# The transfers that place the transposed blocks of the probabilities: begun by GpSimd instead of SyncE

## The chip, the core and the metric

The kernel runs on one core of one Trainium2 chip. The metric is device time in microseconds from one launch. The core has TensorE (PE in the profile), VectorE (DVE), ScalarE (ACT), GpSimd (POOL) and SyncE (SP). Each of them works through its own list of instructions in order and waits on semaphores for what the others produce. Transfers (DMAs) are begun by one of these engines and are carried out by sixteen DMA engines.

## The reference

An attention over chunks of 64 positions is followed by two feed-forward blocks. All in float32.

```python
# q, k, v: (8 batches, 8 heads, 576 positions, 64); nine chunks of 64 positions each
scores = q_c @ k_c^T / sqrt(64)           # 64 x 64 for each chunk and head
attn = exp(scores - max) / (sum + 1e-9)
x = attn @ v_c                            # -> (4608 tokens, 512)
x = ((x @ w1) * (x @ w2)) @ w3 @ w_out    # d_ff 1024
h = x @ w_in                              # d_ff 2048
out = (max(h, 0) + alpha * min(h, 0)) @ w_out2
```

## The kernel before

The 4608 tokens are cut into nine blocks of 512 (`TB`). Attention is done in 18 units of 256 tokens (`u`, two for a block, each unit with 16 pairs of a head pair and a chunk). A matrix product is made of three passes over high and low halves of the operands (`mm3`), so that TensorE does three 128x128 by 512 matmuls for each tile. `proj1` makes the two products with w1 and w2 (into the PSUM banks `a` and `b`), `product` multiplies them, `proj_wc` multiplies by w3 and w_out, folded into one matrix, and sums in `acc`. The last stage (`proj2`, `proj_out`) is the second block.

Attention of the first six units stands in a start phase with an order written out by hand. From unit 6 on (`BLOCKS_FROM`) the units are placed between the projections, two units for each of six blocks of tokens, and each unit has four steps (`unit_steps`):

- `first`: 64 small matmuls for the scores (tile `sc`), their maximum on VectorE, the exponentials on ScalarE (tile `e`).
- `second`: sums, reciprocal and the scaling of `e` on VectorE.
- `third`: `attn_turn(u)`, then the loads of the next unit (`load_unit`, lines 243 and 253).
- `fourth`: 64 small matmuls with the values (`attn_values_by_chunk`, tile `xo`, out of `pt` and `v`), and copies of the result.

`attn_turn` transposes `e` on VectorE, which turns each 32x32 block in place (STREAM_TRANSPOSE, one instruction for the unit). The blocks then stand on the wrong partitions. Eight transfers from SBUF to SBUF, each 32 partitions by 512 float32 (64 KB), carry them to the tile `pt`, of which there is one buffer. For unit u the order on TensorE between the turn and `xo` is the three groups of twelve matmuls (`acc`, `a`, `b`) of the projections around it: for blocks 3 to 7, `third` is placed ahead of the projections of f = 1 or 5, `fourth` behind `proj1` of f = 2 or 6.

TensorE keeps its program order throughout. Before the change all of the kernel's transfers are begun by SyncE, in one list; a scheduler that works with its own estimates of time sets the order on that list. Besides the eight of the turn there are in the same stretch the loads of `qk` and `v` of the next unit, the raw weights of the second block (`raw<-in_w2nd`, line 153, 512 KB each), their converted halves written to memory (`w_dram<-wm`, line 193) and the sums of a block (`y_dram<-y`, line 423). In the lists of instructions a transfer begun by SyncE waits on, and counts up, one of eight semaphores DMAHW0 to DMAHW7 in turn.

Of the kernel before, what the change touches and what calls it, by code (L numbers as in the profile page):

```python
# [60 lines left out]
def tile_attention_moe_moe(ctx: ExitStack, tc: tile.TileContext, qkv: bass.AP, w12: bass.AP,  # L61
# [8 lines left out]
    nc = tc.nc  # L70
# [5 lines left out]
    D = 64  # L76
# [220 lines left out]
    def e_blocks(u):  # L297

        return un[u]["e"].rearrange("p j a h k -> p j (a h k)").rearrange("p k (n x) -> p k n x", n=16)
# [25 lines left out]
    def attn_turn(u):  # L325


        e = e_blocks(u).rearrange("p k n x -> p k (n x)")
        flat = e.rearrange("p k c -> p (k c)")
        dve.transpose(out=flat, in_=flat)  # L330
        pt = un[u]["pt"] = work.tile([P, 2, 4 * 2 * 2, D // 2], F32, tag="pt", name="pt", bufs=1)
        for c in range(2):
            for i in range(2):
                for k in range(2):
                    r, to = D * c + D // 2 * i, D * c + D // 2 * k
                    nc.sync.dma_start(out=pt[to:to + D // 2, i].rearrange("p n x -> p (n x)"), in_=e[r:r + D // 2, k])  # L336

    def attn_values_by_chunk(u):
        v, pt = un[u]["v"].rearrange("p j a (h d) -> p j a h d", h=2), un[u]["pt"]
# [149 lines left out]
    for step in STARTUP.split():  # L489
        kind, rest = step[0], [int(n) for n in step[1:].split(".")]  # L490
        n = rest[0]
# [34 lines left out]
    def unit_steps(u, cut):  # L526


        def first():
            attn_scores(u)  # L530
            attn_max(u)
            attn_exp(u, range(1 if cut else 2))

        def second():
            if cut:
                attn_exp(u, range(1, 2))
            attn_softmax(u)

        def third():
            attn_turn(u)  # L540
            if u + 1 < NU:
                load_unit(u + 1)

        def fourth():
            attn_values_by_chunk(u)
            attn_out(u, False)
            attn_out(u, True)
        return [first, second, third, fourth]
# [110 lines left out]
```

## Time and profile before

| | |
|---|---|
| median of three runs | 1506.35 us (1504.86 to 1507.29) |
| time of the profiled execution | 1505.47 us |
| its span, first to last instruction | 1503.7 us |
| TensorE busy | 1478.7 us, 98% of the span |
| VectorE, ScalarE busy | 805.8 us (54%), 409.2 us (27%) |
| GpSimd busy | 0.7 us, 6 instructions |
| transfers of the turn (`pt<-e`) | 96 of 64 KB, 12 units by 8 |
| stretch in which they lie | 241.6 to 631.2 us of the span |

The span is what the profile sees; the 1.8 us between it and the execution's time lie around it. Busy time of TensorE is modelled for pipelined matmuls, so what matters is where TensorE sat idle and what ended the idle time. In the views a start is in us from the start of the span, and a value in square brackets is the time that the engine was idle before the row, with what ended it. SPq is SyncE's list of transfers; the length of its rows is the time to begin them, not to move the data. Line 105 is a helper through which most compute instructions are recorded, so tiles are told apart by name.

### The profile page before, as it was taken

The page shows a single profiled execution, that of the slowest core. Times are in us where ns is not written, and L with a number is a line of the kernel's source. Part 1 is how long each engine was busy: PE and PEld are TensorE (multiplying, and loading weights), DVE is VectorE, ACT ScalarE, POOL GpSimd, SP SyncE. Part 2 cuts the span into 40 slices and gives each one's busy share as a digit, 9 for nine tenths or more (in the row PEclk, how much of TensorE's full clock was granted, in tenths as well). Part 3 has the DMA queues.
Part 4 walks back from the last instruction along what each step waited for, and adds up shares of the span by engine and source line. Part 5 has one row for each costly group of instructions (what it writes and reads, how often), then busy time and mean ns, then how long its engine had stood idle before and what let it go on. Part 6 is the DMA issues. An engine that isn't in the chain of part 4 may idle for free.

```text
span 1503.7 us, 21181 instructions
## 1 busy us (share of the span) xinstructions
PE 1478.7 (98%) x8592; PEld 1218.1 (81%) x8592; DVE 805.8 (54%) x1274; ACT 409.2 (27%) x1108; POOL 0.7 (0%) x6
## 2 busy tenths in 40 slices
PE   5999999999999999999999999999999999999998
PEld 4788887788888888888888888888888888888887
DVE  7999984376666666622434343443434344343433
ACT  6554334344443444321111111111111111111111
POOL 0000000000000000000000000000000000000000
PEclk9999999999999999999999999999999999999999
DMA  8544447465555555565201010000101000000000
GB/s 296 175 141 153 150 153 230 136 210 169 169 168 146 174 180 180 184 240 194 78 0 56 1 56 1 28 29 0 56 1 56 0 15 28 0 29 1 28 0 28
DMA packets 78992, 148.18 MB, mean 99 GB/s; under 512 B 33072, under 2 KB 35120, under 8 KB 78896
## 3 DMA queue, kind: packets, MB, share of 16 engines
q1 hardware_dynamic: 78896, 146.84, 30.3%
q8 instruction: 67, 1.10, 0.3%
q14 instruction: 29, 0.24, 0.0%
HBM read 98.57 MB, written 41.94 MB: 93 GB/s over the span
## 4 chain that ended last, share of the span: by engine, by line
PE 92%; DVE 4%; ACT 2%; DMA 1%; SPq 1%; issue 0%; ACTq 0%; DVEq 0%
PE acc L105 38%; PE b L105 23%; PE a L105 23%; PE ab L105 3%; DVE m L105 2%; PE wc L105 1%; ACT e L105 1%; DVE p L105 1%; PE xo L105 1%; PE sc L105 1%; PE pa L105 1%; DMA raw<-in_w 0%; SPq L253 0%; DVE w L105 0%; SPq L336 0%
## 5 line engine op out<-in xcount | busy, mean ns | idle before, releaser
L105 PE MATMUL acc<-w,gs 128*128 128x512 f32 x1728 | 414.7, 389 | 0.0
L105 PEld LDWEIGHTS acc<-w,gs 128*128 128x128 f32 x1728 | 324.3, 188 | 67.3
L105 ACT CAST gs<-g 128x512 fp32r<-128x512 f32 x168 | 104.4, 623 | 667.5 <-DVE g L105 635.0
L105 PE MATMUL acc<-gs,wc 128*128 128x512 f32 x864 | 207.7, 392 | 1.9 <-ACT y L105 1.1
L105 PE MATMUL b<-y,w 128*128 128x512 f32 x864 | 207.5, 389 | 0.0
L105 PE MATMUL a<-y,w 128*128 128x512 f32 x864 | 207.5, 389 | 0.0
L105 PEld LDWEIGHTS acc<-gs,wc 128*128 128x128 f32 x864 | 160.7, 188 | 37.6 <-DVE gs L105 1.9
L105 PEld LDWEIGHTS a<-y,w 128*128 128x128 f32 x864 | 162.2, 188 | 33.7
L105 PEld LDWEIGHTS b<-y,w 128*128 128x128 f32 x864 | 162.1, 188 | 33.7
L105 DVE TENSOR_TENSOR gs<-g,gs 128x512 fp32r<-128x512 f32 x168 | 115.9, 692 | 134.0 <-ACT gs L105 134.0
L105 PE MATMUL a<-x,wa 128*128 128x512 f32 x720 | 173.5, 390 | 1.4 <-DVE x L105 1.4
L105 PE MATMUL b<-x,wa 128*128 128x512 f32 x720 | 174.7, 391 | 0.1
L105 PEld LDWEIGHTS a<-x,wa 128*128 128x128 f32 x720 | 134.7, 188 | 29.8 <-DVE x L105 1.8
L105 PEld LDWEIGHTS b<-x,wa 128*128 128x128 f32 x720 | 134.2, 188 | 28.8 <-DVE wa L105 0.5
L105 DVE TENSOR_SCALAR g<-b,alpha_sb 128x512 f32<-128x512 f32 x72 | 54.0, 750 | 177.7 <-PE b L105 177.7
L105 DVE TENSOR_SCALAR g<-a,alpha_sb 128x512 f32<-128x512 f32 x72 | 54.0, 750 | 162.6 <-PE a L105 162.6
L105 ACT ACTIVATE e<-sc,mx 128x64 f32<-128x64 f32 x288 | 85.4, 347 | 29.0 <-issue 16.5
L105 DVE TENSOR_SCALAR m<-m 128x512 f32<-128x512 f32 (+1 forms) x144 | 60.8, 423 | 52.1 <-ACT m L105 50.5
L105 DVE TENSOR_TENSOR a<-b,a 128x512 f32<-128x512 f32 x60 | 41.1, 685 | 74.6 <-PE b L105 69.8
L105 ACT ACTIVATION_READ_ACCUMULATOR e<-sc,mx 128x1 f32 x288 | 69.3, 241 | 0.0
L105 ACT COPY a<-a 128x512 f32<-128x512 f32 x60 | 35.9, 598 | 120.1 <-PE a L105 102.3
L105 PE MATMUL ab<-x,wa 128*128 128x512 f32 x288 | 68.5, 392 | 0.0
(60 smaller groups left out, 959.5 us busy)
## 6 DMA issues: line engine op xcount, KB each, us to landing
qk<-in_qkv SPq DMA_DIRECT2D x36, 512.0 KB, 6.1
raw<-in_w2nd SPq DMA_DIRECT2D x32, 512.0 KB, 4.9
w_dram<-wm SPq DMA_DIRECT2D x32, 512.0 KB, 5.4
w<-w_dram SPq DMA_DIRECT2D x32, 512.0 KB, 3.4
y_dram<-y SPq DMA_DIRECT2D x36, 256.0 KB, 3.0
yraw<-y_dram SPq DMA_DIRECT2D x18, 512.0 KB, 4.5
out<-o SPq DMA_DIRECT2D x36, 256.0 KB, 2.1
raw<-in_w SPq DMA_DIRECT2D x16, 512.0 KB, 4.2
```

The lines of the kernel that those rows point to most:

```text
L105: ins = op(*args, **kw)
```

## The change

The eight `dma_start` of `attn_turn` are called on GpSimd instead of SyncE. Shapes, sources and destinations stay.

```diff
@@ attn_turn
             for i in range(2):
                 for k in range(2):
                     r, to = D * c + D // 2 * i, D * c + D // 2 * k
-                    nc.sync.dma_start(out=pt[to:to + D // 2, i].rearrange("p n x -> p (n x)"), in_=e[r:r + D // 2, k])
+                    nc.gpsimd.dma_start(out=pt[to:to + D // 2, i].rearrange("p n x -> p (n x)"), in_=e[r:r + D // 2, k])
```

On GpSimd, whose list held only the constants and the identity matrix of the start, the 96 transfers follow one another (rows with + are new):

```order
 masks.py:199 ISA
 masks.py:199 AFFINE_SELECT ident<-ident 128x128
+L336 DMA pt<-e 32x512 x96
 L656 UNCONDITIONAL_BRANCH
 L656 ISA
```

Nothing else stands on GpSimd's list between the first and the last of them. On SyncE, here at unit 8 (the first unit of the steady part), the eight leave their place between the sums of block 2 and the weights of the second block:

```order
 L193 DMA w_dram_0_115<-wm 128x1024
 L423 DMA y_dram_108<-y 128x512 x3
-L336 DMA pt<-e 32x512 x8
 L153 DMA raw<-in_w2nd 128x1024
 L193 DMA w_dram_1_116<-wm 128x1024
 L153 DMA raw<-in_w2nd 128x1024
 L193 DMA w_dram_0_117<-wm 128x1024
-L253 DMA v<-in_qkv 64x4x64 x6
+L253 DMA v<-in_qkv 64x4x64 x8
```

What stood behind the eight on SyncE now follows directly on what stood ahead of them. The order on TensorE, VectorE and ScalarE is the same as before. What changes on TensorE is what its instructions wait for; here the first `xo` matmuls of unit 6 with their semaphores (DMASW0 to DMASW7 are those of GpSimd's eight transfers):

```order
 L105 MATMUL acc<-gs,wc 128x512 x10
-L105 MATMUL xo<-pt,v 64x64 [waits DMAHW3_49,DMAHW4_49,DMAHW2_49,DMAHW7_49,DMAHW1_49,PE_49]
+L105 MATMUL xo<-pt,v 64x64 [waits DMASW2_49,DMASW3_49,DMASW1_49,DMAHW7_49,DMASW0_49,PE_49]
 L105 MATMUL xo<-pt,v 64x64 [waits DMAHW0_49]
-L105 MATMUL xo<-pt,v 64x64 [waits DMAHW6_49,DMAHW7_49,DMAHW5_49,DMAHW0_49]
-L105 MATMUL xo<-pt,v 64x64 x29
+L105 MATMUL xo<-pt,v 64x64 [waits DMASW7_49,DMASW6_49,DMAHW1_49,DMASW5_49,DMASW4_49]
+L105 MATMUL xo<-pt,v 64x64 [waits DMAHW2_49]
+L105 MATMUL xo<-pt,v 64x64 x12
```

The first `xo` matmul waits for four of the eight transfers and the third for the other four, before and after; the loads of `v` are now waited for by name where they were covered by later transfers of the same list.

## Rows read from the trace of the kernel before

**Rows 1.** The page: span, and busy time by engine.

```profile
span 1503.7 us, 21181 instructions
PE 1478.7 (98%) x8592; PEld 1218.1 (81%) x8592; DVE 805.8 (54%) x1274; ACT 409.2 (27%) x1108; POOL 0.7 (0%) x6
```

**Rows 2.** The page: the chain that ended last, shares by engine.

```profile
PE 92%; DVE 4%; ACT 2%; DMA 1%; SPq 1%; issue 0%; ACTq 0%; DVEq 0%
```

**Rows 3.** Window of turns: length, busy PE PEld DVE ACT POOL, clock, DMA, GB/s.

```profile
236.00:640.00 404.00, 401.54 (x3108) 328.53 (x3107) 249.19 (x428) 166.64 (x560) 0.00 (x0) 1.00 0.56 173
```

**Rows 4.** What TensorE waited for there: total us, times, longest us.

```profile
PE xo L105 <- DMA pt<-e: 1.4, 1, 1.4
PE acc L105 <- ACT y L105: 1.1, 1, 1.1
```

**Rows 5.** The instructions of tile pt: issue ns min/median/max, and landing.

```profile
L336 SPq DMA_DIRECT2D pt<-e x96: 513/588/1367, 241.6 to 631.2; - x96
...
DMA to landing us min/median/max: 1.9/2.0/3.4
```

**Rows 6.** Timeline of unit 6, the first: start, length, engine, tile.

```profile
240.31 1.24 DVE L105 STREAM_TRANSPOSE e<-e 128x1024 f32<-128x1024 f32 x1
241.61 5.03 SPq L336 DMA_DIRECT2D pt<-e  x8
...
246.43 0.33 PE L105 MATMUL xo<-pt,v 64*64 64x64 f32 x4
...
248.15 1.15 PE L105 MATMUL xo<-pt,v 64*64 64x64 f32 x60 [1.39 <-DMA pt<-e]
```

**Rows 7.** Timeline of unit 7.

```profile
272.50 5.00 SPq L336 DMA_DIRECT2D pt<-e  x8
...
279.35 1.02 PEld L105 LDWEIGHTS xo<-pt,v 64*64 64x64 f32 x64 [0.35 <-issue]
```

**Rows 8.** Timeline of unit 8, the first of the steady part.

```profile
309.72 1.24 DVE L105 STREAM_TRANSPOSE e<-e 128x1024 f32<-128x1024 f32 x1
...
310.99 5.01 SPq L336 DMA_DIRECT2D pt<-e  x8
...
316.10 0.53 SPq L153 DMA_DIRECT2D raw<-in_w2nd  x1
...
317.47 1.18 PE L105 MATMUL xo<-pt,v 64*64 64x64 f32 x64
```

**Rows 9.** Timeline of unit 9.

```profile
343.66 5.25 SPq L336 DMA_DIRECT2D pt<-e  x8
...
352.77 1.16 PE L105 MATMUL xo<-pt,v 64*64 64x64 f32 x64
```

**Rows 10.** Timeline of unit 17, the last of the twelve.

```profile
626.82 4.96 SPq L336 DMA_DIRECT2D pt<-e  x8
...
635.01 1.16 PE L105 MATMUL xo<-pt,v 64*64 64x64 f32 x64
```

**Rows 11.** VectorE, 236 to 640 us, by form: count, busy us, mean ns.

```profile
L105 DVE SCALAR_TENSOR_TENSOR m<-raw,m 128x512 uint32<-128x512 uint32 x32 | 22.1, 692 | 1.0
...
L105 DVE TENSOR_SCALAR m<-m 128x512 f32<-128x512 f32 x32 | 13.6, 424 | 49.4 <-ACT m L105 49.4
L105 DVE TENSOR_SCALAR m<-m 128x512 uint32<-128x512 uint32 x32 | 13.4, 419 | 0.1
...
L105 DVE TENSOR_SCALAR p<-m 128x512 uint32<-128x512 uint32 x32 | 13.3, 416 | 0.2
```

**Rows 12.** Scores of the first unit and of unit 7; a window of the first.

```profile
4.55 2.38 PE L105 MATMUL sc<-qk 64*64 64x64 f32 x64 [4.55 <-DMA qk<-in_qkv]
...
257.63 1.16 PE L105 MATMUL sc<-qk 64*64 64x64 f32 x64
...
4.50:7.00 2.50, 2.27 (x64) 1.90 (x64) 0.00 (x1) 0.00 (x0) 0.00 (x0) 1.00 0.91 280
```

**Rows 13.** Timeline of TensorE: one group of twelve of the projections, unit 16.

```profile
594.19 2.88 PE L105 MATMUL a<-x,wa 128*128 128x512 f32 x12
```

## The prediction

> **What bounds the kernel now.** I read the page first. TensorE is busy for 98% of the span and GpSimd runs six instructions in all [rows 1]; the chain that ended last is 92% TensorE [rows 2]. So a change elsewhere shows in the time only where it makes TensorE wait, or ends a wait. The second view is the busy time of the stretch in which the 96 transfers of the turn lie, 236 to 640 us: TensorE is busy for 401.54 of 404.00 us [rows 3]. The idle 2.46 us are nearly used up by two waits, one of 1.4 us for `pt<-e` and one of 1.1 us for a copy on ScalarE [rows 4]. Behind 640 us no turn is left. A gain from this change can therefore hardly be over 1.4 us, 0.1% of the time; a loss has no such ceiling, since TensorE keeps its order and has nothing to do in place of an `xo` that isn't ready.
>
> The third view is the timeline of each unit, for the room that the transfers have. I call room the time from the start of the first of the eight issues to the first `xo` matmul that is not held. Unit 6: 248.15 - 241.61 = 6.54 us, and here TensorE waits, so 6.54 us is also how long SyncE's eight take to be all in place [rows 6]. That agrees with the issues' own rows: eight issues in 5.0 us are 0.63 us apart, and the last lands 2.0 us after its start [rows 5, 6]: 7 x 0.63 + 2.0 = 6.4. Unit 7 has 6.85 us [rows 7], unit 8 has 6.48 [rows 8], unit 9 has 9.11, the most [rows 9], and the last, unit 17, has 8.19 [rows 10]. The twelve rooms, taken the same way, sum to 93.27 us, 7.77 in the mean. Against 6.5 us the transfers are in time by 1.3 us in the mean, and in units 6 to 8 by nothing or by 0.35. This thin cover is what the change leans on.
>
> **What is removed.** SyncE loses 96 issues of 0.588 us [rows 5], 56 us of its time. It is 1% of the chain [rows 2], and what stands behind the eight (raw weights and the halves written to memory, for the last stage) is wanted only hundreds of us later. I cost this at nothing; the cover is that distance. Nor do the eight start earlier. SyncE was already waiting for VectorE's transpose: in unit 8 it ends at 309.72 + 1.24 = 310.96 and the first issue starts at 310.99 [rows 8], in unit 6 at 241.55 and 241.61 [rows 6]. GpSimd waits for the same instruction. That GpSimd's list is empty thus gains nothing.
>
> **What is added.** Eight issues for a unit on GpSimd, one after the other, and the landing of the last. Let L be the time from the transpose's end to the last landing. TensorE waits in each unit for L minus its room, if that is positive; over 9.11 us the total is 12 L - 93.27, against which the 1.4 us of unit 6 are already counted in its room. Nothing on TensorE later absorbs it, as the idle time [rows 3] shows.
>
> No row of before has a transfer begun by GpSimd, so I bound its pace by the nearest rows, SyncE's own of the same 64 KB [rows 5]. Shortest issue 0.513 and shortest landing 1.9: L = 7 x 0.513 + 1.9 = 5.5 us, all rooms are kept and unit 6 gains 1.4 us: 1504.1. Longest issue 1.367 and longest landing 3.4: L = 7 x 1.367 + 3.4 = 12.97 us, so 12 x 12.97 - 93.27 = 62.4 us: 1567.9. Between them I take the middle of the issue rows, 0.94 us, since no row says to which end another engine is nearer. For the landing I take the long end, 3.4 us: SyncE's next transfers of 512 KB, which stood behind the eight (the one of unit 8 starts at 316.10, after them [rows 8]), can now run beside them on the same DMA engines. L = 7 x 0.94 + 3.4 = 9.98 us, and 12 x 9.98 - 93.27 = 26.5 us, some 2.2 us a unit. On the profiled execution's 1505.47 us this is 1532.0. The median of the runs is 0.9 us above that execution, so the forecast for the median is 1533.
>
> The Trainium skill, page "DMA: Bandwidth & Descriptors", section "Specifications", gives about 1 us to the first byte for a transfer begun by GpSimd and about 0.6 for one begun by SyncE, and its section "Issuing engines are not separate DMA queues" says that beginning transfers on several engines saves only the time to begin them. By these alone, as an estimate, L would be 6.9 us, the waits would grow by under 1 us in units 6 to 8, and the time would not change by what can be measured.
>
> The new waits for `v` by name on TensorE I cost at nothing: those loads are begun a whole unit earlier, and only their names change. If a satisfied wait costs issue time, it is a small part of the 0.35 us of issue that already stands ahead of an `xo` [rows 7].
>
> **The rivals.** *Not slower.* GpSimd begins transfers nearly as fast as SyncE. What decides is L = 7.6 us: there the waits are 1.06 in unit 6, 0.75 in unit 7, 1.12 in unit 8 and some hundredths in two units with 7.56, 3.0 us in all, which is 0.2% of the time, about what a measurement of this kernel can tell from no change. With the usual landing of 2.0 us that is an issue every 0.8 us, against SyncE's 0.63. For it: SyncE's rows have 0.588 as their median, so 0.8 leaves a third more. Against it: the cover is used up in units 6 to 8 already, so any delay there counts. Time 1504 to 1509.
>
> *VectorE holds GpSimd back.* If the beginning of a transfer has to wait for some of VectorE's instructions, the issues stretch with the work around them. In the stretch VectorE runs 96 TENSOR_SCALAR of 128x512 at some 420 ns, while other instructions of that shape take 692 [rows 11]; these shorter ones are 0.24 per us, 2.4 in a window of 10 us, and each waited for to its end costs up to 0.42 us: 1.0 us a unit, L = 11, 38.7 us, 1545. For it: VectorE is busy for 249 of 404 us [rows 3], and the window of a turn is full of these conversions. Against it: VectorE's own order says nothing of a link to GpSimd. The Trainium skill states such a link in the page "SBUF — State Buffer", section "SBUF: two separate sides": while VectorE runs an instruction in a mode that takes both ports, GpSimd can't write the descriptors of its transfers. It is the rule that speaks most against the change, and no run so far shows it.
>
> *The clock falls in the new waits.* TensorE's first 64 matmuls of scores, after 4.55 idle us, take 2.38 us, the same 64 of a later unit 1.16 [rows 12]: half the pace, as at 1.2 GHz instead of 2.4, though the granted clock reads 1.00 (the higher level) in that window too. If a wait of 2 or 3 us a unit brings the slow pace back, it costs 1.2 us for the `xo` and up to 2.9 for one group of twelve [rows 13], 4.1 x 12 = 49 us on top of 26: 1582. Against it: behind the wait of 1.4 us in unit 6 the 60 `xo` matmuls still take 1.15 us [rows 6].
>
> *Faster* has no mechanism over 1.4 us.
>
> **How the numbers follow.** Lateness that TensorE waits for, L between 7.6 and 12.97: 0.62, likeliest 1533, own range 1509 to 1569. Not slower, 1504 to 1509: 0.21. VectorE holds the issues back, 1545 and up to some 1570: 0.08. The clock, 1582: 0.07. Something unforeseen that makes it faster by over 0.2%: 0.02. The range reaches down to include the case without change, and up past the long bound of 1568 to a part of the clock's case: 1504 to 1575, which leaves out about 0.1. Faster 0.02, same 0.21, slower 0.62 + 0.08 + 0.07 = 0.77.
>
> **What would show it.** In the profile of the changed kernel, the eight rows `pt<-e` stand on GpSimd's list, and their first start is within 0.2 us of the transpose's end. Their spacing and the landing give L directly; at 0.94 and 3.4 I am right for the right reason, and at 0.8 or less the first rival holds. The waits of TensorE have `xo` on `DMA pt<-e` in ten to twelve units, 26 us in total and 2.2 each, and the busy time of 236 to 640 falls to about 401.5 in 430. The `xo` matmuls themselves keep 1.16 us for 64; 2.3 would be the clock. The prediction is wrong if TensorE's waits for `pt<-e` stay under 3 us, if the issues are much over 1.4 us apart, or if time goes to units in which `pt` was in place.

## The result, and the profile after

| | before | changed |
|---|---|---|
| median | 1506.82 us (4 runs, 1504.86 to 1508.63) | 1521.47 us (4 runs, 1520.13 to 1526.35) |
| ratio | | 1.0107, 95% interval 1.0095 to 1.0120 |
| profiled execution, its span | 1505.47 us, 1503.7 us | 1526.35 us, 1524.6 us |
| TensorE busy, idle in the span | 1478.7 us, 25.0 us | 1486.5 us, 38.1 us |

The change makes the kernel slower by 1.1%, 14.65 us in the medians. The profiled execution is the longest of the four; why it is 5 us over the median is a part of the story. The page of the changed kernel, its span, its busy time by engine and the new queue:

```profile
span 1524.6 us, 21279 instructions
PE 1486.5 (97%) x8592; PEld 1223.4 (80%) x8592; DVE 806.5 (53%) x1274; ACT 410.5 (27%) x1108; POOL 48.6 (3%) x102
q0 software_dynamic: 3072, 6.30, 1.6%
```

Against [rows 1] TensorE is idle for 13.1 us more and busy for 7.8 us more, with the same 8592 matmuls. So two things are lost: waits, and matmuls that take longer. Of the latter some 3 us are the waits' as well: an `xo` group that a wait splits counts 0.33 + 1.15 us [rows 6], a whole one 1.16 [rows 9], and ten are split, against one before. What TensorE waited for in the stretch of the turns, and the transfers of tile `pt` (answers to [rows 4] and [rows 5]; a landing is counted from the start of the transfer's row until the data are in place):

```profile
PE xo L105 <- DMA pt<-e: 12.3, 10, 3.0
PE acc L105 <- DVE gs L105: 1.5, 1, 1.5
PE acc L105 <- ACT y L105: 1.1, 1, 1.1
L336 POOL DMA_DIRECT2D pt<-e x96: 496/496/711, 243.4 to 650.2; - x96
DMA to landing us min/median/max: 1.8/4.4/6.8
```

The one wait of 1.4 us for `pt<-e` has become ten with 12.3 us in total. GpSimd is not slow: its issues take 0.496 us, less than SyncE's 0.588. It is the landing that went from 2.0 to 4.4 us in the median, and from 3.4 to 6.8 at the longest. Where, the timelines of units 6, 7 and 8 show (against [rows 6] to [rows 8]); the two landing rows are those of unit 6 and of unit 7:

```profile
241.56 1.24 DVE L105 STREAM_TRANSPOSE e<-e 128x1024 f32<-128x1024 f32 x1
243.44 4.05 POOL L336 DMA_DIRECT2D pt<-e  x8 [242.14 <-ACT gs L105]
247.18 2.49 SPq L423 DMA_DIRECT2D y_dram<-y  x4
249.51 1.15 PE L105 MATMUL xo<-pt,v 64*64 64x64 f32 x60 [1.48 <-DMA pt<-e]
DMA to landing us min/median/max: 1.8/2.0/2.3
...
272.57 1.24 DVE L105 STREAM_TRANSPOSE e<-e 128x1024 f32<-128x1024 f32 x1
274.41 2.50 SPq L423 DMA_DIRECT2D y_dram<-y  x4
274.43 3.91 POOL L336 DMA_DIRECT2D pt<-e  x8 [26.93 <-DVE y L105]
276.96 3.65 SPq L433 DMA_DIRECT2D g<-g_dram  x4
284.07 1.97 PE L105 MATMUL xo<-pt,v 64*64 64x64 f32 x60 [3.00 <-DMA pt<-e]
DMA to landing us min/median/max: 3.2/4.4/6.0
...
317.28 1.24 DVE L105 STREAM_TRANSPOSE e<-e 128x1024 f32<-128x1024 f32 x1
319.14 3.91 POOL L336 DMA_DIRECT2D pt<-e  x8 [40.80 <-DVE a L105]
319.71 0.33 SPq L153 DMA_DIRECT2D raw<-in_w2nd  x1
321.52 0.32 SPq L193 DMA_DIRECT2D w_dram<-wm  x1
327.19 1.28 PE L105 MATMUL xo<-pt,v 64*64 64x64 f32 x60 [1.74 <-DMA pt<-e]
```

In unit 6 SyncE begins nothing between the transpose's end (242.80) and 247.18, and GpSimd's eight land in 2.0 us, as SyncE's did. In unit 7 SyncE writes four sums and loads four products (256 KB each) beside them, and the same eight take 3.2 to 6.0 us. In unit 8 it is a load of 512 KB at 319.71 and a store at 321.52, which before could start only behind the eight, at 316.10 in [rows 8]. The reader is to see that the wait follows SyncE's rows, not GpSimd's. Between the transpose's end and the first `xo` not held lie 6.7 us in unit 6, 10.3 in unit 7 (284.07 - 273.81) and 8.7 in unit 8 (327.19 - 318.52); before it was 6.5 to 6.9 in these three.

The rest of the second loss shows in windows (columns as in [rows 3]); the first three rows are of the changed kernel, behind the waits of unit 7 and of unit 8 and while unit 8's eight are under way, the last of the kernel before, unit 8:

```profile
284.00:290.00 6.00, 5.92 (x70) 4.97 (x71) 1.98 (x3) 1.30 (x3) 0.00 (x0) 0.50 0.27 72
328.10:331.40 3.30, 3.30 (x22) 2.60 (x13) 1.75 (x4) 1.11 (x3) 0.00 (x0) 0.50 0.49 167
319.10:327.20 8.10, 6.31 (x32) 4.87 (x30) 7.93 (x15) 2.92 (x5) 3.91 (x8) 1.00 0.80 237
311.00:317.40 6.40, 6.40 (x29) 5.07 (x27) 6.26 (x12) 2.30 (x4) 0.00 (x0) 1.00 0.38 89
```

Behind the wait of 3.0 us the granted clock is 0.50 (1.2 GHz instead of 2.4), and 60 `xo` matmuls take 1.97 us, not 1.15. The low reading lasts from 283.7 to 290.5 and, behind unit 8's wait of 1.74 us, from 328.1 to 331.4. At half the pace these 10.1 us cost up to 5 us, an estimate; with the 3 us of the split groups that is the 7.8 us of longer busy time. And while unit 8's eight are under way the DMA engines are busy for 0.80 of the time, against 0.38 before.

### The profile page after: what moved, and what is told of

The parts are those of the page before. It is cut to its first block, busy times and chain, and to the rows that moved or that the text cites. A ratio compares the mean times of both kernels' runs of the same rounds, so it can differ in the third digit from the quotient of the medians.

```text
span 1524.6 us, 21279 instructions
## 1 busy us (share of the span) xinstructions
PE 1486.5 (97%) x8592; PEld 1223.4 (80%) x8592; DVE 806.5 (53%) x1274; ACT 410.5 (27%) x1108; POOL 48.6 (3%) x102
## 4 chain that ended last, share of the span: by engine, by line
PE 56%; ACT 0%; DVE 0%; DMA 0%; issue 0%; POOL 0%; DVEq 0%
PE acc L105 28%; PE b L105 14%; PE a L105 14%; ACT e L105 0%; DMA pt<-e 0%; POOL pt L336 0%; DVE e L105 0%; DVE gs L105 0%; PE xo L105 0%; ACT y L105 0%; DVE o L105 0%; ACT o L105 0%; DVE y L105 0%; DVE p L105 0%; DVE sm L105 0%
## 5 line engine op out<-in xcount | busy, mean ns | idle before, releaser
L105 PE MATMUL acc<-gs,wc 128*128 128x512 f32 x864 | 211.5, 397 | 3.0 <-DVE gs L105 1.8
```

The source lines that it names most:

```text
L105: ins = op(*args, **kw)
```

## The experiments

Two theories stood at the start. Theory 1, neighbours: on one list the turn's eight kept SyncE's large transfers behind them; on two lists these run beside them on the same DMA engines, and the small ones land late. Theory 2: GpSimd's own path is late, or VectorE holds it back. Times are medians, ratios are to the kernel before on the same chip.

**All of it on GpSimd.** The change, and SyncE's neighbours moved as well:

```diff
-  nc.sync.dma_start(out=pt[...], in_=e[...])
+  nc.gpsimd.dma_start(out=pt[...], in_=e[...])
...
-  nc.sync.dma_start(out=raw, in_=...)
+  (nc.gpsimd if w == "m" else nc.sync).dma_start(out=raw, in_=...)
...
-  nc.sync.dma_start(out=w2_dram[f, half], in_=...)
+  nc.gpsimd.dma_start(out=w2_dram[f, half], in_=...)
...
-  nc.sync.dma_start(out=to(i), in_=t)
+  (nc.gpsimd if name == "y" else nc.sync).dma_start(out=to(i), in_=t)
...
-  nc.sync.dma_start(out=g, in_=g_dram[b, f])
+  nc.gpsimd.dma_start(out=g, in_=g_dram[b, f])
```

`w == "m"` are the raw weights of the second block, `name == "y"` the sums. The loads of `qk` and `v` and those of the last stage stay on SyncE.

> Theory 1 (neighbours): the transfers of the turn land late because SyncE's transfers of 256 and 512 KB, which stood behind them on one list, now run beside them. Here the raw weights of the second block, their halves written to memory, the sums and the products are begun by GpSimd too, so that they stand behind the turn's eight again. Expected: landing of pt<-e back to about 2.0 us in the median (4.4 in the changed kernel), TensorE's waits for it under 4 us in total, time 1505 to 1510. Theory 2 (GpSimd's own path, or VectorE's instructions that hold it back): VectorE's work is the same, so landing stays at about 4.4 us, waits at 12 us or more, time 1518 or more.

1505.61 us (10 runs), ratio 0.9998 (0.9989 to 1.0008): the whole loss is gone. Transfers of `pt` and TensorE's waits, then unit 8:

```profile
L336 POOL DMA_DIRECT2D pt<-e x96: 496/498/706, 241.2 to 631.0; - x96
DMA to landing us min/median/max: 1.8/1.9/4.3
PE xo L105 <- DMA pt<-e: 1.5, 2, 1.0
...
308.65 1.23 DVE L105 STREAM_TRANSPOSE e<-e 128x1024 f32<-128x1024 f32 x1
310.45 3.94 POOL L336 DMA_DIRECT2D pt<-e  x8 [1.97 <-issue]
314.38 0.59 POOL L153 DMA_DIRECT2D raw<-in_w2nd  x1
316.33 1.16 PE L105 MATMUL xo<-pt,v 64*64 64x64 f32 x64
```

With the 512 KB load behind the eight again, GpSimd's transfers land in 1.9 us in the median. The longest, 4.3 us, is in unit 17 (eight issues from 627.58), where a load of 512 KB for the last stage, still on SyncE, begins at 628.83. VectorE's work is the same, so it does not make the transfers land late. Theory 2 falls as the cause of the loss. One row stays unexplained: behind the fifth of unit 12's eight GpSimd's list stands still for 2.67 us (452.96 to 455.63) with nothing in the profile that ends the pause, and the wait of 1.0 us is behind it. Whether VectorE has to do with that pause is not shown.

**The other way round.** The turn stays on SyncE; the four neighbours above go to GpSimd.

> The turn's transfers stay on SyncE; the raw weights, their halves, the sums and the products are begun by GpSimd. Theory 1 (neighbours): it takes only two lists, whichever has the turn, so landing of pt<-e on SyncE rises from 2.0 to about 4 us in the median, and TensorE waits 8 us or more for it; time 1512 to 1525. Theory 2 (GpSimd's own path is late): landing stays at 2.0, the waits at 1.4 us, time within 0.2% of before.

1524.10 us, ratio 1.0117 (1.0100 to 1.0133), as slow as the change. Transfers, waits, and unit 7:

```profile
L336 SPq DMA_DIRECT2D pt<-e x96: 520/588/1624, 240.4 to 651.6; - x96
DMA to landing us min/median/max: 1.9/3.6/8.4
PE xo L105 <- DMA pt<-e: 15.2, 11, 5.4
...
272.20 6.52 SPq L336 DMA_DIRECT2D pt<-e  x8
273.01 2.22 POOL L423 DMA_DIRECT2D y_dram<-y  x4 [18.79 <-DVE y L105]
275.22 2.15 POOL L433 DMA_DIRECT2D g<-g_dram  x4
284.96 1.97 PE L105 MATMUL xo<-pt,v 64*64 64x64 f32 x60 [5.44 <-DMA pt<-e]
```

The turn's transfers, on their old engine, are late as soon as the large ones stand on another list (3.6 us in the median, 8.4 at the longest). It is the two lists, not the engine.

**The turn by ScalarE.** As the change, with `nc.scalar` for `nc.gpsimd`.

> The turn's transfers are begun by ScalarE; GpSimd begins none. Theory 1 (two lists side by side, whichever engines have them): SyncE's large transfers again run beside the turn, so landing of pt<-e goes over 3 us in the median with a longest one over 4.5, and TensorE waits 8 us or more for it, besides what ScalarE loses by the 5 us of issues in each unit; time 1515 to 1535. Theory 2 (GpSimd is needed on one of the two lists): landing stays at 2.0 with a longest one of 3.4, waits for pt under 4 us; time 1506 to 1512, what is over 1506 being ScalarE's.

1520.81 us, ratio 1.0101 (1.0086 to 1.0116). Transfers and waits:

```profile
L336 ACTq DMA_DIRECT2D pt<-e x96: 514/602/1597, 242.5 to 643.8; - x96
DMA to landing us min/median/max: 1.9/2.6/5.1
PE acc L105 <- ACT y L105: 6.1, 2, 5.6
PE xo L105 <- DMA pt<-e: 3.7, 3, 1.8
```

Half a miss. Landing does grow, to 5.1 at the longest, with no GpSimd in it; but its median is 2.6, not over 3, and the waits for `pt` are 3.7 us, not 8 (theory 2 gave under 4). The trace says why the median is low: the neighbours are fewer. In units 10 and 15 SyncE begins no large transfer beside the eight (in the changed kernel it begins one in each), and these land in 2.0 us in the median with a longest one of 2.0 and 2.5. In the eight units with a load of 512 KB beside them (8, 9, 11 to 14, 16 and 17) the median is 3.7 to 4.2 us. So the same run shows both cases, which speaks for theory 1. Of the rest of the loss 5 us are ScalarE's own: in unit 7 it stands at its eight issues while TensorE waits 5.6 us for a copy of sums that is behind them. Behind that wait the granted clock is 0.50 from 279.3 to 286.0, and TensorE's busy time is 3.7 us longer than before.

**Half and half.** Four transfers (`c = 0`) on SyncE, four on GpSimd.

```diff
-                    nc.sync.dma_start(out=pt[...], in_=e[...])
+                    (nc.gpsimd if c else nc.sync).dma_start(out=pt[...], in_=e[...])
```

> Four of the eight transfers (c = 0) on SyncE, four (c = 1) on GpSimd. Theory 1 (neighbours): SyncE is busy with its four for 2.5 us after the turn, GpSimd's four are begun by then and run beside nothing large; landing about 2 us for both, all eight in place some 4.7 us after the transpose against 6.5, no wait of TensorE, time 0 to 2 us under before. Theory 2 (GpSimd's path or VectorE): GpSimd's four land 4 us or more after their issue, all in place after 6 to 7 us, waits of 1 to 4 us in units 6 to 8, time at or up to 4 us over before.

1505.55 us (10 runs), ratio 0.9993 (0.9984 to 1.0003): not told apart from before. No wait of TensorE for `pt` is left, not even unit 6's. Landing is 2.3 us in the median and 4.5 at the longest (expected 2): a neighbour still meets some of the eight, but with four in a row on each list they are in place in time all the same. The gain of up to 2 us that theory 1 allowed does not show.

**No neighbours in units 8 to 17.** The change, with most of the raw loads and the stores of the halves left out:

```diff
...
+            if w == "m" and i >= 43:
+                conv_raw[i] = conv_raw[40 + (i - 40) % 3]
+                return
...
-            nc.sync.dma_start(out=w2_dram[f, half], in_=w_g.pop(conv[i]).bitcast(F32))
+            g = w_g.pop(conv[i])
+            if f == 0:
+                nc.sync.dma_start(out=w2_dram[f, half], in_=g.bitcast(F32))
...
-            nc.sync.dma_start(out=g.bitcast(F32), in_=w2_dram[f, half])
+            nc.sync.dma_start(out=g.bitcast(F32), in_=w2_dram[0, half])
```

> The changed kernel, with 29 of the 32 loads of raw weights of the second block and 30 of the 32 stores of their halves left out (the conversion works on the first three raw tiles over and over, and the last stage reads the first tile's halves for all). VectorE's work stays. Theory 1 (neighbours): in units 8 to 17 nothing large runs beside the turn except the sums in some units: landing about 2.0 in the median, waits of TensorE only in units 6 and 7 (1.5 and 3.0 us) and where sums are written; total 3 to 7 us, time 1507 to 1513. Theory 2 (VectorE holds GpSimd back): VectorE's instructions are the same: landing 4.4, waits 12 us or more.

1513.11 us, ratio 1.0047 (1.0031 to 1.0062). Landing and waits:

```profile
DMA to landing us min/median/max: 1.8/2.0/6.1
PE xo L105 <- DMA pt<-e: 5.2, 4, 2.6
284.00:290.00 6.00, 6.00 (x70) 5.01 (x67) 1.87 (x3) 1.07 (x2) 0.00 (x0) 0.50 0.28 73
```

The waits are in units 6, 7, 8 and 17, and the time is 0.1 us over what theory 1 gave. Unit 8 still has one of the two halves that are stored (at 321.18), unit 17 a load of 512 KB for the last stage (at 636.84) beside its eight. A part of the time is not the turn's: the granted clock is also 0.50 from 232.2 to 235.5, ahead of the first turn, behind a wait of 1.9 us for `gs`. Landing is back at 2.0 with GpSimd's list and VectorE's work as in the change. Unit 7 keeps its neighbours, its wait of 2.6 us and the clock of 0.50 behind it.

**Units 6 and 7 alone.** The change, with the sums and the products on GpSimd too; raw weights and halves stay on SyncE.

> The changed kernel, with the loads of the products and the writing of the sums begun by GpSimd too, behind the turn; the raw weights and their halves stay on SyncE. These were the only neighbours in units 6 and 7. Theory 1: landing in units 6 and 7 goes to about 2 us, unit 7's wait of 3.0 us goes, and with it the stretch at half the granted clock behind it; units 8 to 17 keep their waits: total 7 to 9 us, granted clock 1.00 in the mean, time 1513 to 1517. If the clock falls for another reason than unit 7's wait, its mean stays at 0.996 and the time is some 5 us more.

1515.55 us, ratio 1.0082 (1.0055 to 1.0109). Landing of units 6 and 7, the waits of all units, and the window where the clock had fallen:

```profile
DMA to landing us min/median/max: 1.8/1.9/2.2
PE xo L105 <- DMA pt<-e: 7.7, 8, 2.0
284.00:290.00 6.00, 6.00 (x27) 4.69 (x26) 3.64 (x6) 3.26 (x6) 0.00 (x0) 1.00 0.76 161
```

Unit 7's wait and the low clock behind it are both gone in this profile; the profiled execution has a mean clock of 1.000 and 1515.23 us, which is 10 us over the kernel before: waits of 7.7 us against 1.4, and 2.8 us more of busy time, about what eight split groups give. One of its four executions still took 1523.87 us at a mean clock of 0.997. The longest wait left is 2.0 us, in unit 8.

**Later use.** The change, with the values two groups of twelve later, in units 8 to 17:

```diff
+            if parts and f % 4 == 3:
+                parts[4 * (f // 4) + 3]()          # behind proj1(b, f, 0)
...
-            if parts and f % 4 == 2:
-                parts[4 * (f // 4) + 3]()          # behind proj1(b, f, 1)
```

> The changed kernel, with the use of pt (values and their copies) put two groups of twelve matmuls later in units 8 to 17, which gives these ten units 5.4 us more room. If the whole loss is lateness against the room, the waits of units 8 to 17 go to zero with landing still at 4 us or more; units 6 and 7 keep their 1.5 and 3.0 us, and what the lower clock costs behind unit 7 stays: total wait 4 to 5 us, time 1509 to 1516. If the loss lay elsewhere (SyncE's list, VectorE, the clock for another reason), the time stays at 1518 or more.

1512.41 us, ratio 1.0055 (1.0038 to 1.0073). Landing stays at 4.3 us in the median, and TensorE waits in units 6 and 7 alone:

```profile
DMA to landing us min/median/max: 1.8/4.3/5.9
PE xo L105 <- DMA pt<-e: 4.9, 2, 2.8
```

So a late landing costs where it exceeds the room, and the ten steady units' loss was lateness. The low clock was expected behind unit 7; here it was behind unit 6.

**The change once more.**

> The changed kernel once more, for a second profile and more times. Waits of TensorE for pt<-e 11 to 16 us, landing 4 to 5 us in the median. If the lower clock behind unit 7 is a matter of chance from one execution to the next, the times spread over 1519 to 1527 with a mean clock between 1.000 and 0.996, the lower clock going with the longer time, some 5 us for 0.004.

1521.83 us, ratio 1.0112 (1.0094 to 1.0129). Waits for `pt` were 10.4 us, 0.6 below the least that was expected, and landing 4.3. The eight executions of the changed kernel, here and in the result, by mean clock: 1.000: 1519.54, 1520.13 and 1520.34 us; 0.998: 1520.16, 1522.60 and 1523.50; 0.995 and 0.996: 1524.91 and 1526.35. So the clock falls in some executions and not in others, for up to 6 us. Without it the loss is 13 to 15 us against the median before on the same chip, and the waits (12.3 - 1.4 us in the first profile, 10.4 - 1.4 in the second) with the split groups (3 us) make up 12 to 14 of that.

## Why the prediction was right, and where its terms were not

*The bound.* TensorE waits, GpSimd's slack is worth nothing, and a loss has no cover: as read. In the profiled execution idle time grew by 13.1 us, 10.9 of it in waits for `pt<-e`.

*What is removed.* The step fell short here. "I cost this at nothing" held for SyncE's own time, and no gain was seen. But the eight issues on SyncE had a use: they kept its large transfers off the DMA engines for the 5 us in which `pt` was under way. Taking them away is the cause of the whole loss: with the neighbours behind the eight again, on GpSimd, the time is that of before (ratio 0.9998). I had it only as a reason for the long landing.

*The start.* GpSimd's first row stands 0.62 us behind the transpose's end (unit 8: 318.52 to 319.14), not 0.2. Since its rows are short it is made up by the eighth.

*The pace, mis-sized.* 0.94 us an issue was expected, 0.49 measured (eight in 3.91 us), below even the short bound of 0.513. Here GpSimd's issues follow one another faster than SyncE's (0.63 us apart).

*The landing, mis-sized the other way.* 3.4 us expected, 4.4 in the median and up to 6.8 measured, over the long bound. The reason given (SyncE's 512 KB beside the eight) was right, though 256 KB do it too (unit 7), and is shown by the moves in both directions; the row I bounded it with came from a list in which little ran beside them.

*The sum.* L was forecast as 9.98 us; the units that waited, other than 6, have 8.6 to 10.3. The two errors cancelled for the greater part, which was luck: by the prediction's own sign, 0.94 and 3.4, the sum was not right for the right reason. What was left counts twelve times: 26.5 us forecast, 14.65 measured. So direction and range held, and the point was 12 us too high. Waits of `xo` in ten to twelve units were forecast and came in ten, but with 12.3 us in total, not 26.

*The rivals.* "Not slower" had its condition, an issue every 0.8 us, more than met; it failed because it assumed the usual landing. "VectorE holds GpSimd back" fell: it would have stretched the issues by 1.0 us a unit, and the eight take 3.9 to 4.4 us in every unit, less than SyncE's 5.0; landing is 1.9 us with the same VectorE work when all stands on one list, and in unit 7 of the changed kernel it reaches 6.0 us though VectorE runs no TENSOR_SCALAR of 128x512 in that window. The Trainium skill's rule of the two ports (page "SBUF — State Buffer", section "SBUF: two separate sides") may hold for other work; no run here shows it. The one long pause of GpSimd's list, 2.67 us in the run with all of it on GpSimd, has no cause in the profile. "The clock falls" came true in part, behind unit 7 and partly 8, where the waits are longest, and cost up to 6 us, not 49.

The Trainium skill's page "DMA: Bandwidth & Descriptors", section "Issuing engines are not separate DMA queues", says that transfers of all engines run on the same DMA engines and interleave. The traces agree in so far as a list of its own does not keep a transfer apart: landing went from 2.0 to 4.4 us. My estimate by that page, no measurable change, left that out.

Open: how the DMA engines share between two lists, such that 64 KB wait so long behind 256 or 512 KB, which wait makes the clock fall in a given execution, and the pause of GpSimd's list in unit 12 of the run with all of it on GpSimd.

## What to carry to other kernels

A single list of transfers is also a schedule: a small transfer that something waits for is safe from a large one that stands behind it. Before moving it to an empty queue, look at what stands behind it now, since that will start at the same moment; move the large ones along, or leave it. And look at landing times, not at the time to issue.

## What was not expected of the hardware

- GpSimd begins a 64 KB SBUF transfer in 0.49 us, against SyncE's 0.59 to 0.63, and with nothing large beside it lands it in the same 1.9 to 2.0 us. Its first row comes later: some 0.6 us behind the transpose's end, SyncE's 0.03 to 0.08.
- Between two lists a transfer of 64 KB took up to 6.8 us (GpSimd's, beside SyncE's), 8.4 (SyncE's, beside GpSimd's) and 5.1 (ScalarE's, beside SyncE's). On the one list of before the median was 2.0 and the longest 3.4.
- A single wait of TensorE of 2.6 to 3.0 us in unit 7 was followed by a window of 6 us at a granted clock of 0.50 (1.2 GHz) in three profiles: the change's two and the one without neighbours. With later use one of 2.8 us was followed by 1.00, and one of 2.1 us, in unit 6, by a window of 6 us at 0.72. Shorter waits had it too: in the second profile of the change one of 1.5 us, in unit 16, was followed by 0.50 from 616.7 to 620.1, while with the sums and the products moved one of 2.0 us, in unit 8, was not.
